# Weight loads issued by ScalarE, and the first weight pair placed behind the copies of transposed probabilities

## The chip, the cores and the metric

The kernel runs on one core of a Trainium2 chip. The metric is the device time of one execution in microseconds. TensorE (PE in the profile) multiplies matrices and PEld is its weight load; VectorE (DVE), ScalarE (ACT) and GpSimd (POOL) work elementwise; SP issues DMA transfers. Each engine takes its instructions in the order in which the built program lists them.

## The reference

The inputs are q, k and v of shape (4, 8, 576, 64), three weights of a gated MLP (512 to 1536 and back), a vector of 512 gains, and two weights of a second MLP (512 to 2048 and back), all float32. The output is 2304 x 512.

```
scores = q @ k.T / sqrt(64), masked to 0 <= query - key < 64
attn   = softmax(scores) @ v                  # heads joined: x is 2304 x 512
xn     = x / sqrt(mean(x*x) + 1e-6) * rms_g
g, val = xn @ w_gate, xn @ w_val
x      = (g * sigmoid(g) * val) @ w_out
h      = x @ w_in
out    = (h * sigmoid(1.702 * h)) @ w_out2
```

## The kernel before

**Tiling.** The 2304 tokens form six blocks of 384, and each block three attention tiles `m` of 128 tokens. Block 0's attention runs first, by itself (the flag `starting`). Then the gated MLP goes over all blocks twice, each pass (`ps_i`) with six of the twelve 128-wide slices `f` of its hidden layer; in the first pass the attention of block j+1 is threaded through the work on block j, in slots of three for each f. The second MLP follows, block by block.

**Products with split operands.** Each activation and each weight is held as a rounded part and a remainder, both in a format that TensorE takes at full rate; a product is three matmuls (rounded x rounded, remainder x rounded, rounded x remainder). Attention itself uses plain float32 matmuls.

**Weight pairs.** Weights come in pairs of two 128 x 512 pieces: for f = 0 and 1 the pairs (gate 0, value 0), (gate 1, value 1), (out 0, out 1), and so on; 34 in all. One pair goes through five places:

1. `w_load` (L110) takes one of three staging buffers `st` and issues two DMAs of 512 KB from SP (L117). The first three pairs are loaded among the loads of Q, K and V (`load_some`, L188).
2. `w_step` (L133): ScalarE converts the two halves of each value in the buffer (L144, L145), ordered behind an instruction of ScalarE that `hold[0]` names.
3. VectorE joins them into `m` in three steps (L146, L147, L150); the last one frees the staging buffer. There is one `m`.
4. `w_half` (L123), called at the start of the next `w_step`: ScalarE rounds `m` into `w[:, 0]` (L128), here called the rounding.
5. VectorE subtracts to get the remainder `w[:, 1]` (L129), which ends the pair.

`w_step` loads ahead so that all three buffers are in use: the load of pair n+3 takes the buffer of pair n.

**Attention of a tile.** `att_Tk` and `att_Tq` transpose K and Q on TensorE; `att_S` makes the scores (L271), VectorE reduces them (L289), ScalarE takes the exponentials (L301), VectorE scales (L313). `att_PT` (L316) transposes the probabilities, four heads for each of e = 0 and 1 (L321), and `to_sbuf` (L232) copies the result out of PSUM on ScalarE (L233). `att_PV` multiplies with V (L336, the value products) and copies to `x` (L344). `rms_sq` and `rms_scale` normalise x, which is then split into its two parts (L385 to L389).

**What sets the order.** The builder plans the instructions of all engines with modelled times and lists them for each engine; an instruction that is ready can pass an earlier one of the program that is not. `tc.issue_after(i)` keeps an instruction behind `i` in the list of the same engine. In block 0, `hold[0]` is the last exponential when the first pair's `w_step(1)` is called (L507, L508), before the loop over `att_PT`; after that it is the last cast of `split_x` (L517), and from block 1 on the newest tanh (L564).

Of the kernel before, what the change touches and what calls it, by code (L numbers as in the profile page):

```python
# [8 lines left out]
F32 = mybir.dt.float32  # L9
# [13 lines left out]
def window_attention__gated_mlp__mlp_kernel(  # L23
# [13 lines left out]
    nc = tc.nc  # L37
# [8 lines left out]
    NHP = H // 2  # L46
# [5 lines left out]
    T0 = TB  # L52
# [46 lines left out]
    w_next = [0, 0]  # L99
# [3 lines left out]
    def w_src(kind, f):  # L103
        c = slice(f * 128, (f + 1) * 128)
        if kind in "gvh":
            w = {"g": w_gate, "v": w_val, "h": w_in2}[kind]
            return w[:, c].bitcast(I32).rearrange("(k p) f -> p k f", p=128)
        return {"o": w_out, "p": w_out2}[kind][c, :].bitcast(I32)

    def w_load(limit):  # L110
        while w_next[0] < min(limit, n_w):
            pair = w_order[w_next[0]]
            w_next[0] += 1
            st = stp.tile([128, 2, 1024], I32, tag="st", name="st")
            for e, (kind, f) in enumerate(pair):
                dst = st[:, e, :].rearrange("p (k f) -> p k f", k=KC) if kind in "gvh" else st[:, e, :]
                nc.sync.dma_start(out=dst, in_=w_src(kind, f))  # L117
            staged.append(st)

    def after(ins):  # L120
        return tc.issue_after(ins) if ins is not None else nullcontext()

    def w_half():  # L123
        if not half:
            return
        pair, w24 = half.pop()
        w = wp.tile([128, 2, 1024], F32R, tag="w", name="w")
        nc.scalar.copy(w[:, 0, :], w24.bitcast(F32))  # L128
        nc.vector.tensor_tensor(w[:, 1, :], w24.bitcast(F32), w[:, 0, :].bitcast(F32), ALU.subtract)  # L129
        for e, key in enumerate(pair):  # L130
            weights[key] = w[:, :, e * 512:(e + 1) * 512]

    def w_step(limit):  # L133
        w_half()
        if w_next[1] >= min(limit, n_w):
            return
        w_load(w_next[1] + 1)
        pair = w_order[w_next[1]]
        w_next[1] += 1
        st = staged.pop(0).rearrange("p e (f two) -> p (e f) two", two=2)  # L140
        lo, hi = st[:, :, 0], st[:, :, 1]
        m = tmp.tile([128, 1024], I32, tag="tmp", name="m")
        with after(hold[0]):
            nc.scalar.mul(hi.bitcast(F32), hi.bitcast(F32), 2.0 ** -112)  # L144
            nc.scalar.activation(lo, lo.bitcast(U32), AF.Copy, scale=2.0 ** -29)  # L145
        nc.vector.tensor_scalar(m.bitcast(U32), hi.bitcast(U32), 3, None, ALU.logical_shift_left)  # L146
        nc.vector.scalar_tensor_tensor(  # L147
            m.bitcast(U32), hi.bitcast(U32), 0x80000000, m.bitcast(U32), ALU.bitwise_and, ALU.bitwise_or
        )
        nc.vector.tensor_tensor(m, m, lo, ALU.add)  # L150
        half.append((pair, m))
        w_load(w_next[1] + 2)


    NLD = 4
# [18 lines left out]
    def part_tile():  # L174
        if not quad:
            t = wp.tile([128, 4, 512], F32, tag="w", name="quad")
            quad.extend(t[:, i, :] for i in range(4))
        return quad.pop(0)
# [29 lines left out]
    def released(key):  # L208
        ld_done.add(key)
        ld_tile.pop(key)  # L210
        load_some()

    hold = [None]
    starting = [True]
# [14 lines left out]
            return mm_p.tile(shape, F32, tag="gv"[i % 2], name="ps_" + kind)  # L229
        return atp.tile(shape, F32, tag="att", name="ps_" + kind)  # L230

    def to_sbuf(dst, src):  # L232
        nc.scalar.copy(dst, src)  # L233

    def att_Tk(m):
        t = ld_tile["k", m]
# [17 lines left out]
        released(("q", m))  # L254

    p_tiles = {}
    last_exp = [None]
    last_pt = [None]
    pt_tiles = {}

    def key_blocks(n):
        return slice(0, 4, 3) if n % 4 == 0 else slice((n - 1) % 4, (n - 1) % 4 + 2)

    def att_S(m):
        QT = qts[m]
        banks = [att_bank("s") for _ in range(2)]
        prev = last_pt[0] if not starting[0] else None
        for hp in range(NHP):
            for g, e in ((0, 0), (0, 1), (1, 0), (1, 1)):
                with after(prev):  # L270
                    prev = nc.tensor.matmul(  # L271
                        banks[e][64 * g:64 * g + 64, hp * 128:(hp + 1) * 128],
                        QT[64 * e:64 * e + 64, hp, 64 * g:64 * g + 64],
                        KT[64 * e:64 * e + 64, hp, key_blocks(2 * m + g), :],
                        start=True,
                        stop=True,
                    ).ins
        first = next((g for g in range(2) if (2 * m + g) % GPB == 0), None)
        mask = masks[:, MASKS.index(((m + 1) % 2, first))].rearrange("p a b -> p (a b)")
        sm = at.tile([128, 3, 2 * NHP], F32, tag="sm", name="sm", bufs=6)  # L280
        if starting[0] and m > 0:
            p = [part_tile().rearrange("p (h t) -> p h t", h=NHP) for _ in range(2)]
        else:
            pp = at.tile([128, 2 * NHP, 128], F32, tag="p", name="p", bufs=1)
            p = [pp[:, e * NHP:(e + 1) * NHP, :] for e in range(2)]
        for e in range(2):
            for hp in range(NHP):
                i = e * NHP + hp
                nc.vector.tensor_tensor_reduce(  # L289
                    p[e][:, hp, :],  # L290
                    banks[e][:, hp * 128:(hp + 1) * 128],
                    mask,
                    op0=ALU.add,
                    op1=ALU.min,
                    scale=-0.125,
                    scalar=3e38,
                    accum_out=sm[:, 0, i:i + 1],
                )
            for hp in range(NHP):
                i = e * NHP + hp  # L300
                last_exp[0] = nc.scalar.activation(  # L301
                    p[e][:, hp, :],
                    p[e][:, hp, :],
                    AF.Exp,
                    bias=sm[:, 0, i:i + 1],
                    scale=-1.0,
                    accum_out=sm[:, 1, i:i + 1],
                ).ins
        for lo, n, pe in [(0, NHP, p[0]), (NHP, NHP, p[1])] if starting[0] else [(0, 2 * NHP, pp)]:
            r = sm[:, 2, lo:lo + n]  # L310
            nc.vector.tensor_scalar(r, sm[:, 1, lo:lo + n], SUM_EPS, None, ALU.add)
            nc.vector.reciprocal(r, r)
            nc.vector.tensor_tensor(pe, pe, r.unsqueeze(2).to_broadcast([128, n, 128]), ALU.mult)  # L313
        p_tiles[m] = p

    def att_PT(m):  # L316
        for e in range(2):
            p = p_tiles[m][e]
            ps = att_bank("t")
            for hp in range(NHP):  # L320
                last_pt[0] = nc.tensor.transpose(ps[:, hp * 128:(hp + 1) * 128], p[:, hp, :], ident).ins  # L321
            if starting[0] and m > 0:
                pt = part_tile().rearrange("p (h t) -> p h t", h=NHP)
            else:
                pt = at.tile([128, NHP, 128], F32, tag="pt", name="pt", bufs=2)
            to_sbuf(pt, ps.rearrange("p (h t) -> p h t", h=NHP))
            pt_tiles[m, e] = pt

    def att_PV(m, x, c0):
        pt = [pt_tiles.pop((m, e)) for e in range(2)]  # L330
        t = [ld_tile["v", 2 * m + g] for g in range(2)]
        ps = att_bank("v").rearrange("p (h t) -> p h t", h=NHP)
        for hp in range(NHP):
            for g in range(2):
                for e in range(2):
                    nc.tensor.matmul(  # L336
                        ps[64 * e:64 * e + 64, hp, 64 * g:64 * g + 64],
                        t[g][:, 2 * hp + e, :],
                        pt[e][:, hp, 64 * g:64 * g + 64],
                        start=True,  # L340
                        stop=True,
                    )
        if m < 2 * T0 // 128:
            nc.scalar.copy(x[:, :, c0:c0 + 128], ps)  # L344
        else:
            nc.vector.tensor_copy(x[:, :, c0:c0 + 128], ps)
        for g in range(2):
            released(("v", 2 * m + g))
# [97 lines left out]
    m = TB // 128  # L446
    for fn in (att_Tk, att_Tq):
        at_slot(0, 0, lambda m=m, fn=fn: held(fn, m))
    for b in range(1, NB):
        for i in range(TB // 128):  # L450
            m = b * TB // 128 + i
# [6 lines left out]
            h = b - 1  # L458
# [12 lines left out]
    if True:  # L471
# [30 lines left out]
        for m in range(T0 // 128):  # L502
            att_S(m)
            if m + 1 < T0 // 128:
                att_Tk(m + 1)
                att_Tq(m + 1)
        hold[0] = last_exp[0]  # L507
        w_step(1)  # L508
        for m in range(T0 // 128):
            att_PT(m)  # L510
            att_PV(m, x, m * 128)
            s4 = rms_sq(x, m * 128, sq)
            pe_hold = rms_scale(x, sq, m * 128, (m + 1) * 128, s4)
# [181 lines left out]
```

## Time and profile before

Three runs took 1028.36, 1029.68 and 1031.18 us; the median is 1029.68 us.

| | profiled execution |
|---|---|
| its time | 1027.21 us |
| its span, first to last instruction | 1025.4 us |
| TensorE busy | 987.4 us (96%) |
| TensorE weight loads busy | 917.1 us (89%) |
| VectorE busy | 517.4 us (50%) |
| ScalarE busy | 408.7 us (40%) |
| mean granted clock of TensorE | 0.979 |
| data moved by DMA | 88.43 MB, mean 86 GB/s |

A share of busy time is a mean over stages with different limits. Matmuls overlap, and their ends are modelled, so a busy TensorE is not TensorE at its peak. The granted clock is a share of 2.4 GHz; 0.50 is the lower level, 1.2 GHz. DMA-issuing instructions stand under SPq with the time that the issue took, not the transfer's.

### The profile page before, as it was taken

How to read it: one execution, taken by the hardware profiler on the slowest of the kernel's cores; microseconds unless marked ns; L12 is line 12 of the kernel's file. 1: busy time of each engine (PE TensorE's matmuls, PEld its weight loads, DVE VectorE, ACT ScalarE, POOL GpSimd, SP SyncE). 2: the span in 40 equal slices, each digit the busy share in tenths (PEclk: the TensorE clock that was granted, in tenths of full speed). 3: DMA queues.
4: the chain of work that ended last, by engine and by line, in shares of the span. 5: the costliest groups of instructions: out<-in, count | busy, mean ns of one | idle time of the engine just before them, and what ended most of it. 6: DMA issues, size and time to landing. Idle time of an engine off the chain costs nothing.

```text
span 1025.4 us, 15454 instructions
## 1 busy us (share of the span) xinstructions
PE 987.4 (96%) x6158; PEld 917.1 (89%) x6158; DVE 517.4 (50%) x1132; ACT 408.7 (40%) x884; POOL 12.2 (1%) x39
## 2 busy tenths in 40 slices
PE   7888999999989999999999999999999999999997
PEld 5877798988989899999999998998989989999996
DVE  5597756655575655656543688332232322322222
ACT  7586654654554333333332365222222222322222
POOL 2000000000000000000000000000000000000000
PEclk9698999999999999999999999999999999999999
DMA  9648644444361512423411352010010000000000
GB/s 233 184 124 212 181 102 133 101 86 135 83 186 42 196 66 87 165 72 122 157 72 63 113 171 77 1 62 1 1 62 1 32 31 1 31 1 1 32 1 31
DMA packets 113320, 88.43 MB, mean 86 GB/s; under 512 B 77664, under 2 KB 104288, under 8 KB 113248
## 3 DMA queue, kind: packets, MB, share of 16 engines
q1 hardware_dynamic: 113248, 87.44, 29.4%
q8 instruction: 48, 0.79, 0.3%
q14 instruction: 24, 0.20, 0.1%
HBM read 68.55 MB, written 18.87 MB: 85 GB/s over the span
## 4 chain that ended last, share of the span: by engine, by line
PE 83%; DVE 6%; ACT 5%; DMA 4%; issue 1%; SPq 0%; POOL 0%; DVEq 0%; ACTq 0%
PE acc L622 20%; PE psh L396 19%; PE acc L531 13%; PE psg L396 12%; PE psv L396 12%; PE ps_s L271 2%; PE ps_v L336 2%; ACT p L301 1%; PE ps_t L321 1%; DMA st<-in_moe_w_in_dram 1%; DMA st<-in_moe_w_val_dram 1%; DVE xraw L377 1%; ACT st L145 1%; DMA o<-x2s 1%; PE ps_r L367 1%
## 5 line engine op out<-in xcount | busy, mean ns | idle before, releaser
L638 DVE TENSOR_TENSOR a<-a,psh 128x384 f32<-128x384 f32 x96 | 53.0, 553 | 201.9 <-ACT a L637 201.9
L396 PE MATMUL psh<-x2h,w 128*128 128x384 f32 x768 | 153.3, 339 | 0.9 <-DVE a L638 0.6
L622 PE MATMUL acc<-w,gh 128*128 128x512 f32 x576 | 152.9, 397 | 0.0
L396 PEld LDWEIGHTS psh<-x2h,w 128*128 128x128 f32 x768 | 137.2, 188 | 4.3 <-DVE a L638 0.9
L637 ACT ACTIVATE a<-psh 128x384 f32<-128x384 f32 x96 | 47.0, 491 | 220.4 <-PE psh L396 217.2
L622 PEld LDWEIGHTS acc<-w,gh 128*128 128x128 f32 x576 | 107.1, 188 | 18.5
L531 PE MATMUL acc<-ah,w 128*128 128x384 f32 x576 | 117.6, 344 | 3.6 <-ACT w L128 3.3
L531 PEld LDWEIGHTS acc<-ah,w 128*128 128x128 f32 x576 | 103.5, 190 | 4.9 <-ACT w L128 3.7
L565 DVE SCALAR_TENSOR_TENSOR a<-a,psg 128x384 f32<-128x384 f32 x72 | 39.7, 552 | 115.5 <-ACT a L562 115.3
L396 PE MATMUL psh<-x2l,w 128*128 128x384 f32 x384 | 86.2, 338 | 0.0
L622 PE MATMUL acc<-w,gl 128*128 128x512 f32 x288 | 85.1, 396 | 0.0
L642 DVE TENSOR_TENSOR gl<-a,gh 128x384 fp32r<-128x384 f32 x96 | 53.4, 557 | 50.5 <-ACT gh L641 42.7
L562 ACT ACTIVATE a<-psg 128x384 f32<-128x384 f32 x72 | 35.1, 487 | 107.7 <-PE psg L396 107.7
L396 PEld LDWEIGHTS psh<-x2l,w 128*128 128x128 f32 x384 | 69.9, 188 | 5.9
L641 ACT CAST gh<-a 128x384 fp32r<-128x384 f32 x96 | 49.3, 513 | 62.5 <-DVE a L638 49.7
L396 PE MATMUL psg<-xh,w 128*128 128x384 f32 x288 | 65.3, 357 | 6.4 <-DVE a L565 2.6
L622 PEld LDWEIGHTS acc<-w,gl 128*128 128x128 f32 x288 | 54.2, 189 | 12.5
L531 PE MATMUL acc<-al,w 128*128 128x384 f32 x288 | 64.8, 343 | 0.0
L572 ACT CAST ah<-a 128x384 fp32r<-128x384 f32 x72 | 36.8, 511 | 70.1 <-DVE a L569 69.9
L396 PE MATMUL psv<-xh,w 128*128 128x384 f32 x288 | 62.9, 346 | 0.0
L396 PEld LDWEIGHTS psg<-xh,w 128*128 128x128 f32 x288 | 51.3, 193 | 11.4 <-DVE a L565 3.6
L301 ACT ACTIVATE p<-p,sm 128x128 f32<-128x128 f32 x128 | 49.6, 391 | 23.6 <-DVE sm L289 23.6
(104 smaller groups left out, 1433.6 us busy)
## 6 DMA issues: line engine op xcount, KB each, us to landing
st<-in_moe_w_out_dram SPq DMA_DIRECT2D x28, 512.0 KB, 4.3
o<-x2s SPq DMA_DIRECT2D x48, 192.0 KB, 3.4
st<-in_moe_w_in_dram SPq DMA_DIRECT2D x16, 512.0 KB, 5.0
st<-in_moe_w_gate_dram SPq DMA_DIRECT2D x12, 512.0 KB, 4.9
st<-in_moe_w_val_dram SPq DMA_DIRECT2D x12, 512.0 KB, 5.6
qkv<-in_v_dram SPq DMA_DIRECT2D x20, 256.0 KB, 4.2
x<-xraw SPq DMA_DIRECT2D x6, 768.0 KB, 4.7
xr<-x SPq DMA_DIRECT2D x6, 768.0 KB, 4.4
```

Of the source, the lines that this page charges most:

```text
L271: prev = nc.tensor.matmul(banks[e][64 * g:64 * g + 64, hp * 128:(hp + 1) * 128], QT[64 * e:64 * e + 64, hp, 64 * g:64 * g + 64], KT[64 * e ...
L301: last_exp[0] = nc.scalar.activation(p[e][:, hp, :], p[e][:, hp, :], AF.Exp, bias=sm[:, 0, i:i + 1], scale=-1.0, accum_out=sm[:, 1, i:i + ...
L396: nc.tensor.matmul(ps[:, :T], w[:, wi, c * 128:(c + 1) * 128], xx[:, c, :T], start=(i == 0), stop=(i == 3 * KC - 1),)
L531: nc.tensor.matmul(acc[c][:, :T], w[:, wi, c * 128:(c + 1) * 128], aa, start=(f == f_lo and pi == 0), stop=(f == f_hi - 1 and pi == 2),)
L562: tanh = nc.scalar.activation(a, psg[:, :T], AF.Tanh, scale=0.5).ins
L565: nc.vector.scalar_tensor_tensor(a, a, 1.0, psg[:, :T], ALU.add, ALU.mult)
L572: nc.scalar.copy(ah, a)
L622: nc.tensor.matmul(acc[c], (gh, gh, gl)[pi][:, c * 128:(c + 1) * 128], w[:, (0, 1, 0)[pi], :], start=(f == 0 and pi == 0), stop=(f == NF2 ...
L637: nc.scalar.activation(a[:, :T], psh[:, :T], AF.Sigmoid, scale=1.702)
L638: nc.vector.tensor_tensor(a[:, :T], a[:, :T], psh[:, :T], ALU.mult)
L641: nc.scalar.copy(gh[:, :T], a[:, :T])
L642: nc.vector.tensor_tensor(gl[:, :T], a[:, :T], gh[:, :T].bitcast(F32), ALU.subtract)
```

## The change

- All weight loads but the first three pairs move from SP to ScalarE's queue. `w_half` issues one pair's load, ordered behind the rounding; `w_step` issues none.
- The first pair's `w_step(1)` moves into the loop over `att_PT`, to its last turn, and its conversions are ordered behind ScalarE's last copy of transposed probabilities (m = 2, e = 0) instead of the last exponential.
- In block 0 the copies for e = 1 are done by VectorE; those for e = 0 stay on ScalarE.

```diff
-    def w_load(limit):
+    def w_load(limit, queue=None):
+        queue = queue or nc.sync
         while w_next[0] < min(limit, n_w):
...
-                nc.sync.dma_start(out=dst, in_=w_src(kind, f))
+                queue.dma_start(out=dst, in_=w_src(kind, f))
             staged.append(st)
...
         w = wp.tile([128, 2, 1024], F32R, tag="w", name="w")
-        nc.scalar.copy(w[:, 0, :], w24.bitcast(F32))
+        cast = nc.scalar.copy(w[:, 0, :], w24.bitcast(F32)).ins
+        with tc.issue_after(cast):
+            w_load(w_next[0] + 1, nc.scalar)
         nc.vector.tensor_tensor(w[:, 1, :], w24.bitcast(F32), w[:, 0, :].bitcast(F32), ALU.subtract)
...
-        w_load(w_next[1] + 1)
         pair = w_order[w_next[1]]
...
         half.append((pair, m))
-        w_load(w_next[1] + 2)
...
-    def to_sbuf(dst, src):
-        nc.scalar.copy(dst, src)
+    def to_sbuf(dst, src, other=False):
+        if other:
+            return nc.vector.tensor_copy(dst, src)
+        return nc.scalar.copy(dst, src)
...
-            to_sbuf(pt, ps.rearrange("p (h t) -> p h t", h=NHP))
+            copy = to_sbuf(pt, ps.rearrange("p (h t) -> p h t", h=NHP), starting[0] and e == 1)
+            if e == 0:
+                last_copy[0] = copy.ins
             pt_tiles[m, e] = pt
...
-        hold[0] = last_exp[0]
-        w_step(1)
         for m in range(T0 // 128):
             att_PT(m)
+            if m == T0 // 128 - 1:
+                hold[0] = last_copy[0]
+                w_step(1)
             att_PV(m, x, m * 128)
```

## Rows read from the trace of the kernel before

**Rows 1.** Stretches: length; busy PE, PEld, DVE, ACT, POOL; clock, DMA share, GB/s.

```profile
0.00:41.00 41.00, 32.40 (x299) 27.59 (x299) 20.55 (x92) 24.09 (x73) 7.89 (x34) 0.75 0.94 203
41.00:117.00 76.00, 64.15 (x519) 57.67 (x518) 61.70 (x144) 55.73 (x126) 0.86 (x1) 0.91 0.66 180
117.00:1025.40 908.40, 890.82 (x5346) 831.80 (x5344) 435.17 (x900) 328.90 (x687) 3.42 (x4) 1.00 0.24 73
```

**Rows 2.** Waits of TensorE, 0 to 120 us: in total, times, longest.

```profile
PE ps_s L271 <- ACT pt L233: 4.3, 1, 4.3
PE acc L531 <- ACT w L128: 3.3, 1, 3.3
```

**Rows 3.** Chain of waits, 20 to 62 us: start, duration, what.

```profile
22.80 1.02 ACT st L144
...
46.88 4.68 DMA st<-in_moe_w_val_dram
...
51.63 1.16 ACT st L144
...
53.85 2.44 ACT p L301 x13
```

**Rows 4.** Copies by line and shape: count, busy us, mean ns, idle before.

```profile
L346 DVE COPY xraw<-ps_v 128x512 f32<-128x512 f32 x12 | 8.2, 684 | 2.0 <-PE ps_v L336 2.0
...
L233 ACT COPY quad<-ps_t 128x512 f32<-128x512 f32 x4 | 2.2, 579 | 0.2 <-PE ps_t L321 0.2
```

**Rows 5.** TensorE's timeline; in brackets its idle time and what ended it.

```profile
19.67 1.26 PE L336 MATMUL ps_v<-pt,quad 128*64 128x64 f32 x30 [1.28 <-ACT pt L233]
...
25.84 1.97 PE L336 MATMUL ps_v<-quad 128*64 128x64 f32 x30 [2.41 <-ACT quad L233]
...
40.93 0.67 PE L396 MATMUL psg<-xh,w 128*128 128x384 f32 x1
...
64.94 1.10 PE L271 MATMUL ps_s<-KT,QT 64*64 64x128 f32 x30
...
84.05 1.98 PE L271 MATMUL ps_s<-KT,QT 64*64 64x128 f32 x30 [4.30 <-ACT pt L233]
```

**Rows 6.** Stretches as in rows 1: granted clock and DMA share at the end.

```profile
20.00:21.00 1.00, 1.00 (x28) 0.88 (x24) 0.86 (x9) 1.00 (x7) 0.00 (x0) 0.78 1.21 258
26.00:31.00 5.00, 5.00 (x46) 4.42 (x46) 2.39 (x2) 2.91 (x5) 0.00 (x0) 0.50 1.18 229
31.00:36.00 5.00, 4.22 (x42) 4.02 (x41) 1.35 (x6) 1.84 (x3) 0.72 (x2) 0.50 0.69 210
74.00:75.00 1.00, 0.98 (x5) 0.98 (x6) 1.00 (x1) 1.00 (x3) 0.00 (x0) 1.00 0.67 152
80.00:81.00 1.00, 0.00 (x0) 0.00 (x0) 0.26 (x1) 0.00 (x0) 0.00 (x0) 1.00 1.25 277
```

**Rows 7.** VectorE's timeline, as rows 5: last step on the first pair.

```profile
28.28 1.23 DVE L129 TENSOR_TENSOR w<-m,w 128x1024 fp32r<-128x1024 f32 x1 [1.11 <-ACT w L128]
```

**Rows 8.** SP's queue: start, time of issue, line, transfer, count.

```profile
46.47 0.37 SPq L117 DMA_DIRECT2D st<-in_moe_w_gate_dram  x1
...
56.29 0.81 SPq L117 DMA_DIRECT2D st<-in_moe_w_out_dram  x2
...
72.18 2.65 SPq L206 DMA_DIRECT2D qkv<-in_v_dram  x4
74.94 0.56 SPq L117 DMA_DIRECT2D st<-in_moe_w_gate_dram  x1
...
79.86 1.71 SPq L117 DMA_DIRECT2D st<-in_moe_w_out_dram  x2
```

**Rows 9.** ScalarE's timeline: start, duration, line, operation; roundings.

```profile
48.45 1.05 ACT L128 CAST w<-m 128x1024 fp32r<-128x1024 f32 x1
...
72.92 1.05 ACT L128 CAST w<-m 128x1024 fp32r<-128x1024 f32 x1
...
83.90 1.05 ACT L128 CAST w<-m 128x1024 fp32r<-128x1024 f32 x1
```

More of the change, by code (lines that the diff above doesn't have):

```diff
@@ L256, in window_attention__gated_mlp__mlp_kernel @@
     p_tiles = {}
-    last_exp = [None]
+    last_copy = [None]
     last_pt = [None]
@@ L300, in att_S @@
                 i = e * NHP + hp
-                last_exp[0] = nc.scalar.activation(
+                nc.scalar.activation(
                     p[e][:, hp, :],
@@ L307, in att_S @@
                     accum_out=sm[:, 1, i:i + 1],
-                ).ins
+                )
         for lo, n, pe in [(0, NHP, p[0]), (NHP, NHP, p[1])] if starting[0] else [(0, 2 * NHP, pp)]:
```

## The prediction

> **Bound now.** I read the share of busy time by stage first. TensorE is busy 890.8 of the 908.4 us from 117 us on, but only 32.4 of the first 41 us and 64.2 of the 76 us between them [rows 1]. So the long tail is fixed, and a change to the start or to the order of weight preparation is worth what it takes from the first 117 us. Then come TensorE's waits up to 120 us: the two longest are both for ScalarE, 4.3 us for a copy of transposed probabilities and 3.3 us for the rounding of a weight pair [rows 2]. Then the chain of waits, in which work on weight pairs stands at both places that matter here: at 22.80 us ScalarE starts the two conversions of the first pair (1.02 us each on the chain, the second one like the first), and only behind them come the copies that TensorE needs; at 46.88 us the chain runs through a weight transfer of 4.68 us into the conversion at 51.63, and from there into the exponentials at 53.85 [rows 3]. Last I read the order of SP's queue, of ScalarE, and TensorE's timeline with its clock.
>
> I number the weight pairs from 0. The execution profiled took 1027.21 us; its span is 1025.4, so 1.8 us lie around it. The median of the three runs, 1029.68, is 2.5 us above it. The differences below are worked out in that execution and then put on the median.
>
> **First pair.** Two instructions of 1.02 us leave the place at 22.80 us, 2.04 us [rows 3]. With the copy for m=1, e=1 on VectorE, ScalarE loses up to 0.58 us more there [rows 4]. TensorE sat idle 2.41 us before the 30 value products at 25.84 us, because ScalarE copied their probabilities last [rows 5]. It can't start these products before its own transposes for m=2, e=0 end, which is where that idle time begins, so the gain is the idle time, -2.4 us, and not the 2.6 that ScalarE saves. Behind it the same work follows in the same order with TensorE at half clock and nearly without a gap (5.00 of 5 us busy from 26 to 31, 4.22 from 31 to 36 [rows 6]), so the gain is carried to the scaled activations. The conversions themselves now stand behind three copies on ScalarE, about 1.5 us later than before. The last step of the pair, which began at 28.28 and took 1.23 us [rows 7], then ends near 31.0; TensorE wants the pair at 40.93 [rows 5] less 2.4, so 7 us of other work hide the move. If the cover is gone, because the conversions now push the copy of the next attention output instead, 2.04 us come back.
>
> **Copies.** Three copies of 128x512 move to VectorE. The nearest row of VectorE is its copy of that shape out of the same memory, 684 ns, against 579 on ScalarE [rows 4]: 0.1 us more each. The first of them feeds the products at 19.67 us, ahead of which TensorE waited 1.28 us [rows 5]. That idle time shrinks, but what is late next is the last block's exponentials, which wait for VectorE's reductions, and the copy can push these by up to its 0.68 us. The second falls where VectorE waits for exponentials. The third can find VectorE in a step of 1.23 us on the first weight pair, of which I leave half to TensorE's other work: 0.6. So the copies cost between 0 and 1.3 us. I take 0, since VectorE's gaps there are about as long as a copy. For start and copies together the bounds are +0.9 (2.04 and 1.3 come back) and -6.5 (the clock, under the rivals).
>
> **Loads.** On SP, a load waited for the last VectorE step on the pair whose buffer it takes, and for everything ahead of it on SP. Now it stands in ScalarE's order behind the rounding of that pair. Pair 7 is where this helps: SP came to it at 74.94 us, after four loads of V which took 2.65 us from 72.18 [rows 8] and were released only by an attention product. The rounding behind which it will stand began at 72.92 [rows 9]. With its issue next to the rounding it is asked for 1.9 us earlier (74.94 less 73.0), and its landing ended the idle time of ScalarE ahead of the longest wait of TensorE, 4.3 us [rows 2]: -1.9 us. Bounds 0 and -3.7, where the 1.8 us for the slow clock behind that wait go too. Pair 4 is where it may hurt: 46.47 before [rows 8], rounding at 48.45 [rows 9], so up to 2.0 us later. In the order of before, its conversion stands ahead of the exponentials, which began 2.2 us after the conversion did [rows 3], and the delay would go to the 3.3 us wait as a whole. But the order is planned with modelled times when the kernel is built; a load that is modelled later can let the exponentials pass, and then 2.2 us come off. Bounds +2.0 and -2.2, about as far on either side, so I take 0. Pair 8 was asked for at 79.86 us and its rounding began at 83.90, late because ScalarE itself waited [rows 8, 9]: up to 4.0 us later. Its weights are used much later, so I take 0 with an upper bound of +4.0.
>
> These sentences the sum does without. No row of before shows a DMA issued by ScalarE. The Trainium skill, page "Perfetto Trace Analysis", section "DVE / Act Engine Instruction (TENSOR_ADD, Activation, etc)", says that a sequencer, once it has pushed an instruction into the engine's wait queue, is ready for the next one. By that, pair 4's load could leave before its rounding begins, and its +2.0 would shrink towards 0.
>
> **Issue cost.** SP took 0.81 us for the two issues of pair 5 and 1.71 for those of pair 8 [rows 8]. The rounding lasts 1.05 us [rows 9]. If ScalarE's queue issues while its engine rounds, an ordinary pair is hidden; if not, 0.81 us stand in front of tanh, copies and exponentials for each of the 8 pairs handled up to 117 us: +6.5. I take nearly whole cover, 0.06 us for each pair, +0.5 us, because the shorter of the two rows fits under the rounding and the longer one stands in a crowded stretch. Behind 117 us ScalarE is busy 328.9 of 908.4 us [rows 1], so the issues there cost nothing even at 0.81. SP loses these loads, and Q, K and V queue no longer behind them; TensorE's two long waits were not for them, so this is 0.
>
> **Sum.** -2.4 - 1.9 + 0 + 0.5 = -3.8 us, which is 1023.4 for the execution profiled and 1025.9 us on the median.
>
> **Rivals.** First, the start keeps the clock. The granted clock fell in the slice from 20 to 21 us (0.78 in that slice), behind the 1.28 us in which TensorE was idle, and the slices from 26 to 36 us stand at half [rows 5, 6]. The 30 score products took 1.10 us at 64.94 and 1.98 at 84.05, behind the long stall [rows 5]: a factor of 0.56. Were the clock full over the 9.2 busy us from 26 to 36, 4.1 us more would come off: 1021.8. For it speaks that VectorE's copy closes the very idle time ahead of the fall; against it that the third block's probabilities still come late and TensorE waits elsewhere.
>
> Second, only the start counts. The landing of pair 7 doesn't move, since the DMA engines were 67% busy in the slice 74 to 75 us and over 100% at 80 us [rows 6], with V, K and Q loads in the same stretch; two more transfers at 73 us make all of them slower. Then the 1.9 falls out: -2.4 + 0.5 = -1.9, 1027.8 us. Against it speaks that the share was lower while the load stood behind those of V. The Trainium skill, page "DMA: Bandwidth & Descriptors", section "Issuing engines are not separate DMA queues", says that transfers of all issuers run on the same 16 engines and that another issuer saves the time of issue alone; where the engines are the limit this gives 1027.8 too, and the four V loads ahead of pair 7 speak for SP's order as the limit instead.
>
> Third, late loads, on the slower side. A load leaves only behind its rounding, the conversions stay planned ahead of exponentials and copies, and ScalarE waits for each landing with the urgent work queued behind. The price is 2.0 us for pair 4 and 4.0 for pair 8, and behind that last, new stall the clock goes: 0.88 us on the next 30 products, as it was behind the 4.3 us stall [rows 5], and by estimate as much on those after them, 1.8. Together 7.8, less 3.8: +4.0, 1033.7 us. It decides as soon as more than 3.8 of these 7.8 us reach TensorE. For it speaks that the chain shows a late landing with exponentials behind it already; against it that the order is planned anew.
>
> **Chances.** Forecast 0.42 (its own range 1022.5 to 1028.5), clock kept 0.12, only the start 0.28, late loads 0.18. A difference under 0.3% (3.1 us) can't be told from none. Faster by more: 0.26 of the forecast's share, 0.12, 0.07 of the third case, together 0.45. Slower by more: 0.12 of the late loads and 0.04 for issues that aren't covered, 0.16. The rest, 0.39, lies between. The range 1020.5 to 1033.5 takes in the clock's case and most of the late loads; their far end, and issues without cover, are left out.
>
> **Signs.** First pair: no conversion between the exponentials and the copies at 22 to 25 us, and the 30 value products begin near 23.4; if later, VectorE's copies held them up. Clock: 1.00 in the slices after 21 us would be the first rival. Loads: pair 7 is asked for 1.9 us earlier against its neighbours, and the 4.3 us wait is shorter by as much; an earlier issue with the same landing is the second rival. Late loads: ScalarE idle for a transfer with exponentials behind it, longer than before. Issue: gaps of 0.8 us or more on ScalarE behind each rounding would show no cover. I am wrong as a whole if the first 117 us don't shrink, or if the stretch behind them changes by over 1 us.

## The result and the profile after

The changed kernel took 1038.18 us (median of six runs, 1034.34 to 1041.91) against 1029.6 us (1026.31 to 1031.18) on the same chip. The ratio is 1.0094, 95% interval 1.0066 to 1.0121: 0.9% slower, where 1025.9 us was forecast, and past the end of the range. The execution profiled is the slowest of its six: 1041.91 us, span 1040.1, against 1027.21 and 1025.4 before, so its differences are read for places rather than for the size. Line numbers are now one to six higher: the rounding is L129, the conversions L146 and L147, the copies L235 (VectorE) and L236 (ScalarE), the value products L341.

The stretches of [rows 1], after:

```profile
0.00:41.00 41.00, 27.70 (x288) 23.68 (x288) 20.93 (x89) 22.07 (x67) 8.31 (x34) 0.76 0.95 203
41.00:117.00 76.00, 63.69 (x512) 57.58 (x513) 60.06 (x142) 55.26 (x125) 0.00 (x0) 0.90 0.65 170
117.00:1040.10 923.10, 898.46 (x5360) 839.60 (x5358) 438.36 (x904) 331.01 (x690) 4.28 (x5) 0.99 0.24 73
```

TensorE lost 4.7 busy us in the first 41. The clock behind 117 us is 0.99 and no longer 1.00; as the first two stretches have a fixed length, the last one holds all 14.7 us of the difference, wherever they arise. Its waits up to 120 us, which answer to [rows 2]:

```profile
PE ps_r L378 <- POOL ry L376: 8.6, 3, 6.9
PE acc L537 <- ACT w L129: 7.3, 3, 4.9
...
PE ps_s L274 <- ACT pt L236: 0.3, 1, 0.3
```

The 4.3 us wait for a copy of probabilities is gone (0.3), but the wait for roundings rose from 3.3 to 7.3, and one of 6.9 us is new. To find where the difference arises I take ScalarE's first stored result `x2s` (c = 0) at the end of each block of the first pass as a mark. The columns are TensorE's first projection, the end of block 0, the lengths of blocks 1 to 5, and the way from there to the second MLP, each in us of one profiled execution (the e numbers are the experiments below).

| kernel | first projection | block 0 ends | 1 | 2 | 3 | 4 | 5 | second pass |
|---|---|---|---|---|---|---|---|---|
| before | 40.93 | 111.7 | 57.7 | 58.0 | 59.2 | 54.9 | 44.5 | 224.7 |
| after | 43.17 | 117.3 | 59.0 | 58.1 | 60.6 | 58.7 | 46.8 | 225.0 |
| e2, queue alone | 40.97 | 113.4 | 59.0 | 57.2 | 60.8 | 59.0 | 46.7 | 225.1 |
| e5 | 39.54 | 110.3 | 60.7 | 58.1 | 60.1 | 55.3 | 46.8 | 224.6 |
| e6 | 39.76 | 110.9 | 58.0 | 57.2 | 59.0 | 54.8 | 44.5 | 224.4 |
| e9 | 40.02 | 109.0 | 57.2 | 58.4 | 58.3 | 56.0 | 44.6 | 224.6 |
| e12, order alone | 41.21 | 112.9 | 60.9 | 57.0 | 61.5 | 58.3 | 55.1 | 224.5 |

After loses 2.2 us up to the first projection, 3.4 more to the end of block 0, and 9.0 in blocks 1 to 5, above all in 4 and 5, though the diff touches no line that only those blocks run.

**Start.** TensorE's timeline (idle time and releaser in brackets), answering to [rows 5]:

```profile
20.25 1.15 PE L341 MATMUL ps_v<-pt,quad 128*64 128x64 f32 x30 [2.03 <-DVE pt L235]
...
25.12 1.97 PE L341 MATMUL ps_v<-quad 128*64 128x64 f32 x30
...
37.78 0.79 PE L378 MATMUL ps_r<-ident,ry 128*128 128x128 f32 x2 [6.91 <-POOL ry L376]
38.36 1.71 PE L372 MATMUL ps_r<-ones,s 128*128 128x1 f32 x8
...
43.17 0.67 PE L401 MATMUL psg<-xh,w 128*128 128x384 f32 x1
```

The products of m = 1 came 0.7 us earlier (25.84 before) and no longer waited, but not at 23.4. Those of m = 0 came 0.6 us later, now behind VectorE's copy. Then the normalisation of m = 1 stood still for 6.91 us. GpSimd is named there, but VectorE's timeline and one step of the chain of waits show who was late:

```profile
34.76 1.12 DVE L382 SCALAR_TENSOR_TENSOR xraw<-xraw,g_sb,ps_r 128x128 f32<-128x128 f32 x4 [5.46 <-DMA g_sb<-in_moe_rms_g_dram]
35.80 1.22 DVE L132 TENSOR_TENSOR w<-m,w 128x1024 fp32r<-128x1024 f32 x1
36.93 0.15 DVE L375 TENSOR_SCALAR rv<-ps_r 128x1 f32<-128x1 f32 x1
```

```profile
25.77 8.88 DMA g_sb<-in_moe_rms_g_dram
```

VectorE was early enough to scale by the gains `g_sb`, and these had not landed: 2 KB, issued by SP behind the first loads of Q, K and V, in flight for 8.88 us. Behind the waiting instruction in VectorE's list stood the moved subtraction (1.22 us) and then `rv`, which TensorE's next step needs. Before, the same load was in flight for 7.1 us and landed at 33.05, ahead of the scaling at 34.57.

The move of the loads seems to have a share in this. On SP, the load of pair 3 stood behind that of the gains and was issued at 29.67; in after it left ScalarE's queue at 28.74. The earlier it left, the longer the gains flew: 10.6 us with pair 3 issued at 27.21 (e2), 8.9 with 28.74, 7.1 with 29.67, 6.6 with 30.87 (e1). No run varies this by itself. And a late landing doesn't cost in every order. In e2, VectorE waited 4.88 us for the gains, and the first projection began at 40.97 all the same. VectorE's and TensorE's timelines in e2:

```profile
36.17 1.12 DVE L378 SCALAR_TENSOR_TENSOR xraw<-xraw,g_sb,ps_r 128x128 f32<-128x128 f32 x4 [4.88 <-DMA g_sb<-in_moe_rms_g_dram]
```

```profile
35.99 1.87 PE L368 MATMUL ps_r<-ones,s 128*128 128x1 f32 x8 [0.78 <-ACT s L354]
38.05 1.55 PE L374 MATMUL ps_r<-ident,ry 128*128 128x128 f32 x4 [0.19 <-POOL ry L372]
```

There, as in the kernel before, TensorE takes the sums for m = 2 (35.99) ahead of the normalisation of m = 1 (38.05); in after they stand behind it (38.36 behind 37.78) and wait too. This is read from the lists; no run tests it alone.

**Loads in block 0.** ScalarE's timeline with the issues of its queue (ACTq), answering to [rows 8, 9], and pair 7's value load from the chains of waits, after and then before:

```profile
48.77 0.37 ACTq L118 DMA_DIRECT2D st<-in_moe_w_gate_dram  x1
...
50.72 1.03 ACT L129 CAST w<-m 128x1024 fp32r<-128x1024 f32 x1
...
74.48 0.39 ACTq L118 DMA_DIRECT2D st<-in_moe_w_gate_dram  x1
...
75.77 1.04 ACT L129 CAST w<-m 128x1024 fp32r<-128x1024 f32 x1
```

```profile
74.91 9.70 DMA st<-in_moe_w_val_dram
```

```profile
75.55 5.80 DMA st<-in_moe_w_val_dram
```

In these rows a load listed behind a rounding leaves 1.3 and 2.0 us ahead of it (others up to 2.25, at 84.80 against 87.05, or with it, at 28.74 against 28.73): the queue goes on while the engine still has to run what it was given. The Trainium skill, page "Perfetto Trace Analysis", section "DVE / Act Engine Instruction (TENSOR_ADD, Activation, etc)", says that a sequencer is ready for the next instruction once it has pushed one into the engine's wait queue, and these rows agree. So pair 7 was asked for at 74.48, 0.5 us earlier than before and not 1.9; it flew longer and landed at 84.61, not 81.35.

**Ends of blocks.** ScalarE's timeline at the end of block 3, before and then in e2 (the queue alone):

```profile
286.56 0.50 ACT L606 ACTIVATE x2s<-acc 128x384 f32<-128x384 f32 x1
290.55 0.51 ACT L387 CAST xh<-xraw 128x384 fp32r<-128x384 f32 x1 [0.68 <-DVE xraw L377]
292.38 0.49 ACT L606 ACTIVATE x2s<-acc 128x384 f32<-128x384 f32 x1 [1.33 <-DMA o<-x2s]
292.77 0.50 ACT L387 CAST xh<-xraw 128x384 fp32r<-128x384 f32 x1
```

```profile
290.33 0.50 ACT L607 ACTIVATE x2s<-acc 128x384 f32<-128x384 f32 x1
296.31 0.49 ACT L607 ACTIVATE x2s<-acc 128x384 f32<-128x384 f32 x1 [2.73 <-DMA o<-x2s]
296.70 0.91 ACT L388 CAST xh<-xraw 128x384 fp32r<-128x384 f32 x2
```

The second `x2s` needs the buffer of the first, so it waits for that one's store (5.37 us in flight in e2). Before, a cast of the next block's rows stands ahead of it in the list; here in e2 and in after, both casts stand behind it, and TensorE can't begin the next block. So it is at the ends of blocks 0, 2 and 3 in both; at the ends of 1 and 4 they come first. The lengths fit this: in e2 the blocks behind such an end, 1, 3 and 4, are 1.3, 1.6 and 4.1 us longer than before, and block 2 is not. The change put DMA issues into another list, and the planner answered with another order at a place that the diff doesn't touch. Stretches around this point, before and then e2 (the granted clock is the third number from the end):

```profile
286.00:293.00 7.00, 4.62 (x51) 3.48 (x53) 5.57 (x12) 4.11 (x8) 0.85 (x1) 1.00 0.77 247
293.00:298.00 5.00, 5.00 (x56) 4.57 (x49) 3.73 (x21) 2.99 (x15) 0.00 (x0) 1.00 0.60 229
```

```profile
290.00:297.00 7.00, 3.00 (x21) 2.16 (x19) 4.69 (x10) 3.52 (x7) 0.85 (x1) 1.00 0.73 244
297.00:302.00 5.00, 4.75 (x38) 3.98 (x39) 4.47 (x22) 2.07 (x9) 0.00 (x0) 0.50 0.62 237
302.00:307.00 5.00, 5.00 (x51) 4.69 (x50) 1.08 (x4) 2.22 (x11) 0.00 (x0) 0.82 0.01 2
```

TensorE is idle for 1.6 us more, and then it runs at half clock, where before it kept the full one: 0.50 and 0.18 of 5 us, 3.4 us more.

### The profile page after: what moved, and what is told of

Same layout as the page of the kernel before. It is cut to its first block, busy times and chain, and to the rows that moved or that the text cites. A ratio compares the mean times of both kernels' runs of the same rounds, so it can differ in the third digit from the quotient of the medians.

```text
span 1040.1 us, 15411 instructions
## 1 busy us (share of the span) xinstructions
PE 989.8 (95%) x6158; PEld 920.9 (89%) x6158; DVE 519.4 (50%) x1135; ACT 408.3 (39%) x881; POOL 12.6 (1%) x39
## 4 chain that ended last, share of the span: by engine, by line
PE 80%; DMA 6%; ACT 5%; DVE 4%; SPq 2%; issue 1%; ACTq 0%; POOL 0%; DVEq 0%
PE acc L628 19%; PE psh L401 19%; PE psg L401 13%; PE acc L537 12%; PE psv L401 12%; DMA o<-x2s 2%; SPq L207 2%; PE ps_s L274 1%; DMA st<-in_moe_w_val_dram 1%; PE ps_v L341 1%; DMA st<-in_moe_w_in_dram 1%; ACT p L304 1%; DMA st<-in_moe_w_out_dram 1%; ACT st L146 1%; ACT st L147 1%
## 5 line engine op out<-in xcount | busy, mean ns | idle before, releaser
L401 PE MATMUL psg<-xh,w 128*128 128x384 f32 x288 | 68.0, 369 | 13.2 <-ACT xh L392 8.4
L401 PEld LDWEIGHTS psg<-xh,w 128*128 128x128 f32 x288 | 54.3, 203 | 17.9 <-ACT xh L392 9.3
```

The lines of the kernel that those rows point to most:

```text
L401: nc.tensor.matmul(ps[:, :T], w[:, wi, c * 128:(c + 1) * 128], xx[:, c, :T], start=(i == 0), stop=(i == 3 * KC - 1),)
```

## The experiments

The theory after this reading: the time goes at two places, the gains' load at the start and the order at the ends of blocks, and the second comes with the queue. Rivals: the copies and the moved pair cost the time themselves; the loads come late or their issues cost; another owner of the queue would do. The ratios are to the kernel before on the same chip, with 95% intervals.

**e1, the start alone.** The changed kernel with its loads on SP as before:

```diff
-        with tc.issue_after(cast):
-            w_load(w_next[0] + 1, nc.scalar)
...
+        w_load(w_next[1] + 1)
         pair = w_order[w_next[1]]
...
         half.append((pair, m))
+        w_load(w_next[1] + 2)
```

> Start of the change alone: first pair moved and copies on VectorE, weight loads on SP as before. Theory G (the start is lost to the gain vector g_sb, which lands at about 34 us with the next tile's norm queued behind it on VectorE): first projection at 43 us as in the changed kernel instead of 40.9, boundaries between blocks as before, so before + 2 us, about 1031.6. Rival L (late weight loads cost the most): start gains what was predicted, 2.4 us, about 1027.2.

1030.97 us, ratio 1.0017 (1.0000 to 1.0033). The wait for `g_sb` was 1.15 us in this execution and the first projection began at 41.01: no gain, and at most a small loss.

**e2, the queue alone.** The kernel before with `w_load(w_next[0] + 1, nc.scalar)` behind the rounding, and both calls of `w_load` out of `w_step`.

> Queue alone: loads behind the rounding on ScalarE, start as before. Theory X (the planner, which now has issues in ScalarE's list, puts the split of the next block's x behind the second stored tile x2s, and this waits for a store): TensorE's waits for xh of about 8 us in the first pass as in the changed kernel, stretch up to 117 us within 2 us of before, time before + 6, about 1035.6. Rival L: the stretch 41 to 117 us grows by 4 us or more, waits for xh as before (2.3 us), time about 1034. Rival D (the issues block ScalarE): gaps of about 0.9 us on ScalarE behind each rounding.

1039.12 us, ratio 1.0094 (1.0076 to 1.0112): as slow as the whole change. Pair 4 was asked for at 46.92, against 46.47 on SP [rows 8]; pair 5 at 56.66, against 56.29. From 41 to 120 us ScalarE waited 3.0 us for weight transfers, against 5.5 before. Late loads are not the reason here. (In after itself it waited 8.0 us, so in its block 0 they can have a share.) The issues take 0.35 to 0.62 us each in block 0 and run beside the engine's work, here a rounding:

```profile
64.72 0.39 ACTq L118 DMA_DIRECT2D st<-in_moe_w_gate_dram  x1
64.77 1.03 ACT L129 CAST w<-m 128x1024 fp32r<-128x1024 f32 x1
```

TensorE's waits for the casts from 100 to 420 us, before and then e2:

```profile
PE psg L396 <- ACT xh L387: 2.3, 3, 0.8
```

```profile
PE psg L397 <- ACT xh L388: 8.0, 4, 3.2
```

**e3, the gains first.** The changed kernel with the load of `g_sb` as ScalarE's first DMA:

```diff
+        nc.scalar.dma_start(out=g_sb, in_=rms_g.rearrange("(k p) -> p k", p=128))
         load_some()
-        nc.sync.dma_start(out=g_sb, in_=rms_g.rearrange("(k p) -> p k", p=128))
```

> Changed kernel with the load of g_sb as the first instruction of ScalarE instead of the last of SP's first loads. Theory G: VectorE's 5.5 us wait for g_sb is gone, first projection at 38.5 to 39 us instead of 43.2, time 4 us under the changed kernel, about 1034. If G is wrong: the wait goes to something else and the first projection stays at 42 to 43 us, time 1038.

1034.52 us, ratio 1.0048 (1.0032 to 1.0064). The load lands 3.8 us after its issue at 0.72, the wait is gone, and the first projection begins at 39.45, 3.7 us earlier than in after. With the changed start, the gains' load is a cause; e2, whose first projection isn't late, loses as much in all.

**e4, the casts first.** The changed kernel with the second `x2s` of ScalarE ordered behind the last cast:

```diff
-                        nc.scalar.mul(st, acc[c][:, :T], 0.5)
+                        with after(xh_last if c == 2 and not end else None):
+                            nc.scalar.mul(st, acc[c][:, :T], 0.5)
```

> Changed kernel with the second stored tile of ScalarE (x2s, c=2) ordered behind the last cast of xh at each block boundary but the last. Theory X: TensorE's waits for xh fall from 8.4 to under 3 us, time 5 to 7 us under the changed kernel, about 1032. Rival L: the waits change places, time within 2 us of 1038.

1034.24 us, ratio 1.0055 (1.0037 to 1.0073). The waits for the casts fell from 8.4 us in after to 3.4, and block 4 from 58.7 to 55.2. Block 5 stayed at 46.9: at its start the tanh (353.14) still stands behind that `x2s` (352.75), which waited 2.75 us for its store.

**e5, both mended**, the edits of e3 and e4 on the changed kernel.

> Changed kernel with both edits of e3 and e4: gains loaded first, second stored tile behind xh. If the two losses are separate, they add: 4.6 + 3.9 us under the changed kernel's 1038.2, about 1029.7. If they share a cause (everything behind the start only shifts), one of the two gains is missing: about 1034.

1032.97 us, ratio 1.0049 (1.0034 to 1.0064): the two gains don't add. The start keeps its gain, but block 1 is now 60.7 us.

**e6, as e5 but with the loads on SP.**

> Weight loads on SP as before; the changed start, gains loaded first, second stored tile behind xh. Theory G: the start now gives the 2.4 us of the prediction, first projection near 38.5 us, and xh waits at the boundaries are gone too: about 1026, 5 us under e1. Rival (the copies on VectorE take back what the first pair gives): first projection at 40 us or later, time 1029.

1026.1 us, ratio 0.9992 (0.9975 to 1.0009). The time came as theory G had it, the first projection (39.76) as its rival had it. With the loads on SP the loss is gone, so some 0.57% stays with the queue even where both places are mended. Block 1 shows 2.7 us of it in the profiled executions. The stretches 110 to 115, 115 to 120 and 120 to 125 us, e5 and then e6:

```profile
110.00:115.00 5.00, 3.00 (x19) 2.07 (x17) 2.90 (x7) 2.35 (x6) 0.86 (x1) 1.00 0.77 166
115.00:120.00 5.00, 4.85 (x38) 3.79 (x39) 4.65 (x24) 1.85 (x9) 0.00 (x0) 0.56 0.62 236
120.00:125.00 5.00, 5.00 (x49) 4.69 (x48) 2.63 (x6) 2.63 (x12) 0.00 (x0) 0.76 0.01 3
```

```profile
110.00:115.00 5.00, 3.72 (x26) 2.97 (x26) 2.33 (x6) 2.50 (x5) 0.86 (x1) 1.00 0.80 160
115.00:120.00 5.00, 4.19 (x45) 2.97 (x45) 5.00 (x14) 2.47 (x6) 0.00 (x0) 1.00 0.95 315
120.00:125.00 5.00, 5.00 (x57) 4.68 (x56) 3.19 (x18) 3.65 (x18) 0.00 (x0) 1.00 0.15 53
```

TensorE is busy for 12.85 us of the 15 in e5 and 12.91 in e6. The difference is the clock: e5 has 2.00 of its 2.15 idle us in the first of these stretches, and behind it loses 0.44 and 0.24 of 5 us, 3.4 us.

Block 5 shows another 2.3 us. ScalarE at its start, e5 and then e6:

```profile
351.48 0.49 ACT L613 ACTIVATE x2s<-acc 128x384 f32<-128x384 f32 x1 [2.76 <-DMA o<-x2s]
351.86 0.48 ACT L568 ACTIVATE a<-psg 128x384 f32<-128x384 f32 x1
```

```profile
346.48 0.49 ACT L568 ACTIVATE a<-psg 128x384 f32<-128x384 f32 x1 [2.24 <-PE psg L401]
...
349.71 0.49 ACT L613 ACTIVATE x2s<-acc 128x384 f32<-128x384 f32 x1 [1.81 <-DMA o<-x2s]
```

With the loads on SP the first tanh passes the waiting `x2s`; with the loads on ScalarE it stands behind it. It looks like the fault of the block ends again, with another instruction behind the wait; no run mends this place alone.

**e7, the kernel before with both edits.**

> Kernel before with the same two edits, none of the change: the control for e6. Theory G: in the kernel before the gains land ahead of their first use, so the early load gives nothing, first projection at 40.9 us; the order of xh gives up to 2 us: 1027.5 to 1029.5. If this is as fast as e6, the changed start is worth nothing.

1028.31 us, ratio 1.0004 (0.9990 to 1.0018). Its first projection begins at 39.83 against 39.76 in e6, so the moved pair and the copies gain little that can be told there; e7's execution was already 0.8 us ahead at the transposes of m = 0 (16.96 against 17.77). VectorE's timeline in e6, and TensorE's products that wait for it:

```profile
20.62 0.69 DVE L235 COPY pt<-ps_t 128x512 f32<-128x512 f32 x1
```

```profile
21.36 1.97 PE L341 MATMUL ps_v<-pt,quad 128*64 128x64 f32 x30 [2.96 <-DVE pt L235]
```

VectorE's list has the copy for m = 0 behind all reductions of the scores of m = 2. In the kernel before these products began at 19.67 [rows 5], in e7 at 18.86. That isn't all. The first scaling by the gains comes 2.1 us earlier in e6 than in e7 (31.35 and 33.48), and what follows up to the first projection takes 8.4 us and not 6.4. In e6 TensorE has the sums of m = 0 ahead of the products of m = 1 (25.62 and 27.26), in e7 behind them (28.09 and 25.03); so the gain went to the first tile's normalisation, and the first projection waits for the last one's.

**e8, the loads on GpSimd's queue**, the kernel before with the edit of e2 and `nc.gpsimd`.

> Kernel before with the weight loads behind the rounding's place in the program, but issued by GpSimd instead of ScalarE. In the list that the builder makes, the casts of xh then stand ahead of the second stored tile in four of five boundaries. Theory X (what the queue costs is the order on ScalarE that its issues bring): waits for xh under 3 us, time within 2 us of before, 1028 to 1031. Rival L (loads asked for later cost by themselves, whatever queue): 1034 or more, with ScalarE's waits for weight transfers in the first 120 us longer than the 5.5 us of before.

1055.47 us, ratio 1.0267 (1.0250 to 1.0285). GpSimd's timeline:

```profile
27.08 0.92 POOL L118 DMA_DIRECT2D st<-in_moe_w_gate_dram  x1 [19.53 <-DVE m L152]
35.64 0.78 POOL L118 DMA_DIRECT2D st<-in_moe_w_val_dram  x1 [7.64 <-issue]
```

GpSimd stands idle for 7.64 us between the two loads of this pair, and the power for the normalisation (36.49) comes behind both. What it waits for there, the profile doesn't show. Neither expectation was met as a whole: TensorE's waits for the casts are 4.8 us, not under 3, and ScalarE's waits for weight transfers up to 120 us are 8.3, above the 5.5 of before, as rival L had it. Loads as late as these do cost, but GpSimd's own gaps made them late, so the run does not decide what ScalarE's queue costs.

**e9, the first copy back.** e6 with the copy for m = 0, e = 1 on ScalarE again:

```diff
-            copy = to_sbuf(pt, ps.rearrange("p (h t) -> p h t", h=NHP), starting[0] and e == 1)
+            copy = to_sbuf(pt, ps.rearrange("p (h t) -> p h t", h=NHP), starting[0] and e == 1 and m > 0)
```

> e6 with the first tile's copy (m=0, e=1) back on ScalarE; the other two copies stay on VectorE. Theory C (VectorE's list puts that copy behind the eight reductions of the third tile, and this eats what the moved pair gave): the 30 value products of m=0 begin near 19 us instead of 21.4, the first projection near 37.6 instead of 39.8, time 2 us under e6, about 1024. Rival (the norms of the three tiles set the end of the start anyway): first projection at 39 us or later, time as e6.

1024.84 us, ratio 0.9967 (0.9952 to 0.9982): the fastest version, and the only one faster than before. Its products for m = 0 begin at 19.92 instead of 21.36, but its first projection (40.02) is no earlier than in e6, as the rival had it. TensorE now waits ahead of the normalisation of m = 0, whose `rv` (27.60) VectorE has behind two steps on the moved pair (25.73 and 26.46):

```profile
29.52 0.80 PE L378 MATMUL ps_r<-ident,ry 128*128 128x128 f32 x2 [2.30 <-POOL ry L376]
```

The gain lies behind the first projection, in the stretch 41 to 117, which has TensorE busier and the clock at 0.95, against 0.91 before [rows 1]:

```profile
41.00:117.00 76.00, 65.92 (x554) 57.87 (x553) 63.61 (x148) 55.73 (x127) 0.86 (x1) 0.95 0.72 191
```

So the edit did what was expected for the products, and the time came in block 0 behind it. Whether the new plan of block 0 or the clock gave it isn't shown.

**e10, all copies back on ScalarE**, otherwise e6.

> e6 with all copies of transposed probabilities on ScalarE: the moved first pair alone, gains early. Theory C: the pair's 2.0 us on ScalarE are gained in full, first projection near 37.8 us, within 1 us of e9. If the copies on VectorE are worth something for m=1 and 2, it comes 0.5 to 1 us later than in e9.

1033.28 us, ratio 1.0063 (1.0049 to 1.0076). Its start is the best of all (first projection 38.99, block 0 ends at 107.3), and the later blocks lose it again: block 5 takes 49.9 us. Its waits from 100 to 420 us have another head, which was 2.6 us before:

```profile
PE psg L401 <- DVE a L571: 9.4, 5, 3.7
```

**e11, a tile of its own** for ScalarE's second `x2s`, on the changed kernel:

```diff
-                    st = stp.tile([128, TB], F32, tag="os", name="x2s", bufs=2)
+                    if c == 2:
+                        st = tmp.tile([128, TB], F32, tag="s4", name="x2s", bufs=1)
+                    else:
+                        st = stp.tile([128, TB], F32, tag="os", name="x2s", bufs=2)
```

> Changed kernel, order of lists as it comes, but ScalarE's second stored tile (x2s, c=2) is written to a tile of its own and so needn't wait for the store of the first. Theory S (what the queue costs is ScalarE's wait for a store in front of urgent work, at all six boundaries): ScalarE's waits for o<-x2s are gone, the last block of the first pass takes 44.5 us instead of 46.8, time 6 to 8 us under the changed kernel, about 1031. Rival (only the place of xh matters, as e4 mended it): 1034.

1040.63 us, ratio 1.0128 (1.0109 to 1.0148): no better. ScalarE no longer waits for a store, but the other three results share two buffers, and VectorE's second one now waits, with the scaling that the casts need (298.34) behind it:

```profile
297.86 0.56 DVE L613 TENSOR_SCALAR x2s<-acc 128x384 f32<-128x384 f32 x1 [3.08 <-DMA st<-in_moe_w_out_dram]
```

The row names a weight transfer as what ended this wait; that it was for the store of the shared buffer is inferred. A wait stayed at this place (TensorE's waits for the casts are 8.9 us), so this run does not test whether the store is needed for the loss.

**e12, the order alone.** The kernel before, loads on SP, with the split of the next block moved behind the storing loop:

```diff
-                        split_x(x, nxh, nxl, T)
-                        x_store(j + 1, x)
...
+                    split_x(x, nxh, nxl, T, last_st)
+                    x_store(j + 1, x)
...
-                last = nc.scalar.copy(xh[:, c, :T], x[:, c, :T]).ins
+                with after(behind):
+                    last = nc.scalar.copy(xh[:, c, :T], x[:, c, :T]).ins
```

> Before kernel, all weight loads on SP as before, start as before; only the list changes: at the end of a block of the first gated pass, the split of the next block's rows (both xh casts of ScalarE, and with them the subtractions and the store of the rows) stands behind ScalarE's second stored result x2s, as the lists of the changed kernel have it in most blocks. Theory O (that order at the block ends costs most of what the queue alone costs, about 10 us): 1033 to 1039 us, with TensorE's waits of psg for ACT xh up from 2.3 us to 8 us or more in 100 to 420. Rival Q (the order is harmless by itself; the place of the loads on ScalarE's queue delays something else): 1028 to 1031 us, waits of psg for xh under 4 us. Between the two, the order is a part of it.

1042.13 us, ratio 1.0127 (1.0098 to 1.0157). The order alone, without any load on ScalarE, costs about as much as the change did or more (the intervals overlap). Waits from 100 to 420 us, and ScalarE's longest wait:

```profile
PE psg L397 <- ACT xh L388: 18.6, 5, 10.3
```

```profile
360.46 0.49 ACT L601 ACTIVATE x2s<-acc 128x384 f32<-128x384 f32 x1 [5.46 <-DMA o<-x2s]
```

The edit puts both casts behind the second `x2s` at all five block ends, where e2 has three, and moves VectorE's part of the split as well. Its block 5 loses more than in any other kernel, and its block 2 nothing (57.0 against 58.0), so it shows what this order can cost, not that it is the whole of e2.

## Why the prediction was wrong

**Bound now.** The step that failed is "So the long tail is fixed, and a change to the start or to the order of weight preparation is worth what it takes from the first 117 us." The reading of the busy shares was right, and yet about 9 of the 15 us between the two profiled executions were lost in blocks 1 to 5. The plan is made anew for the whole kernel, and a stall at the end of a block can also cost the clock behind it (0.50 behind 4.0 idle us of 7 in e2). The working knew of the new plan, but only for pair 4. Both of its signs of being wrong as a whole came: block 0 ended 5.7 us later, and the stretch behind it grew by more than 1 us. e2 shows that the queue brings the loss and e12 that the order at the block ends can make one as large; e4 gives 0.4% of it back, and e5 and e6 show that 0.57% (6.9 us between their medians) stays with the queue when both places are mended: 2.7 us of it in block 1, where the clock fell, and 2.3 in block 5, where the tanh stands behind the same `x2s`; these two places are read from the traces, not tested. The rest, and why the planner orders so, stays open.

**First pair, -2.4 us.** The idle time before the products of m = 1 did go (2.41 us to none), but they began 0.7 us earlier and not 2.4, and nothing reached the first projection. What was late next was not looked for far enough: the load of the gains, 1.5 us of margin before (33.05 against 34.57), which no row of the sum held. The subtraction that was said to be hidden by "7 us of other work" stood behind that wait, ahead of the `rv` that TensorE needed. e3 shows it: 3.7 us back. Even so the 2.4 us didn't reach the first projection: "behind it the same work follows in the same order" failed. The first scaling came earlier (31.35 in e6, 34.57 before), but TensorE's list now served the normalisation of m = 0 first, and the last tile came no earlier.

**Copies, 0 between 0 and 1.3.** Mis-sized. "VectorE's gaps there are about as long as a copy" reckoned with an instruction that takes the first gap; VectorE takes its list in order, and the list has the first copy behind the reductions of m = 2. It held the products back to 21.36 in e6 against 19.67 before, 1.7 us, more than the bound. It is not the only thing that took the start's gain: with that copy back on ScalarE (e9) the first projection was no earlier, and TensorE waited 2.30 us elsewhere. The working did name what could be late next, with the order reversed: it feared that the copy would push the reductions.

**Loads.** Pair 7's -1.9 failed: the issue moved by 0.5 us in after. The 4.3 us wait did go, and came back as 4.9 for a rounding. Pair 4 at 0 was right (0.45 us later in e2), pair 8 was 1.7 us later there (81.52, against 79.86), and with them the rival of late loads falls for e2, though its price, 1033.7 us, was the nearest to the result. That price lay just outside a range that was said to take in most of this case.

**Issue cost, +0.5.** Nearly whole cover was right: the issues run beside the engine's work (e2). Nine pairs, not eight, were rounded up to 117 us, so its price without cover would have been 7.3 us and not 6.5.

**The rivals.** The clock was not kept (0.76 in the first 41 us, 0.75 before). "Only the start counts" forecast a gain that e1 doesn't show, though its condition, that pair 7 lands no earlier, held in after (84.61 against 81.35) and nearly in e2 (80.96). The cause of the loss in e2 was none of the three.

## What to carry to other kernels

Where a planner sets the order, compare the order of each engine's list far from the edit as well, above all where a wait for a store or load can stand ahead of the work that starts the next stage; the price of an edit at its own place says nothing on that. When an idle time is to go, look up when each later input lands, tiny transfers too, and put these ahead of the bulk. An engine that has a gap takes a moved instruction only if its list has it there.

## What the runs showed of the hardware

- A 2 KB load took 6.6 us (e1) to 10.6 us (e2) to land when issued behind the bulk loads, 3.5 to 4.0 us of it SP's issue, and 3.8 us as the first DMA of ScalarE's queue (e3).
- About the same idle time of TensorE cost the clock in one execution and not in another: 2.15 us of it from 110 to 120 us, 2.00 before 115, were followed by a clock of 0.56 and 0.76 (e5); 2.09 us, 1.28 before 115 and 0.81 behind, went with 1.00 throughout (e6).
- The first four loads issued by GpSimd took 0.76 to 0.92 us each to issue and stood 8.6 and 4.6 us apart within their pairs (e8); with the same edit on ScalarE's queue a load took 0.35 to 0.62 us in block 0, and the first two pairs stood 0.5 and 0.4 us apart within (e2).
- DMA issues of ScalarE's queue left 0 to 2.25 us ahead of the rounding that they are listed behind, in the first six pairs (28.74 against 28.73 and 84.80 against 87.05, after).
